# Even and odd rows in the filter's first transform, and Q's second half projected last

## The chip, the cores and the metric

The kernel runs on one core of one Trainium2 chip. The metric is the device time of one execution in microseconds. Durations of single instructions come from one profiled execution, whose page and trace are read below.

The core has five engines that run their own instruction lists and meet at semaphores: PE (TensorE, matmuls), ACT (ScalarE), DVE (VectorE), POOL (GpSimd) and SP (SyncE, which here only issues transfers).

## The reference

Two independent computations share one output row: 640 columns of a spectral filter (A) and 640 columns of attention (B).

```python
def _A_ref(x, w_r, w_i):                     # x: (1, 2048, 640); w: (2048, 321)
    X = rfft2(x.astype(float32), axes=(-2, -1))
    X = X * (w_r + 1j * w_i)
    return irfft2(X, s=(2048, 640), axes=(-2, -1)).astype(bfloat16)

def _B_ref(x, wqkv, wo):                     # H = 32 heads of Dh = 20
    q, k, v = heads(x @ wqkv)
    p = softmax(einsum("bhqd,bhkd->bhqk", q, k) * Dh ** -0.5)
    return merge(einsum("bhqk,bhkd->bhqd", p, v)) @ wo

return concatenate([a, b], axis=-1)          # (1, 2048, 1280)
```

## The kernel before

**Attention.** Queries are cut into four chunks of 512 (qc), heads into eight groups of four (g). One pair (qc, g) is a unit; there are 32 units, in the order of the list UNITS: the first 16 have qc 0 and 1, the last 16 have qc 2 and 3. Unit 8 is (0, 4), unit 10 is (0, 6). A unit has 16 key tiles times 4 heads = 64 score tiles, each one matmul of 32 rows by 512 columns (`score_mm`, L821), so there are 2048 score tiles in all. The exponential of a tile is taken on one of two engines. ScalarE takes two tiles in one instruction (L1418). VectorE makes an approximation from integer arithmetic in sets of four tiles (L955 out of PSUM, then L998 and L997 on the set, L1005 on V). P times V is L1076: four 32-column matmuls run side by side as one wave. At a unit's end the sum is copied out (L1107) and normalised by way of two small DRAM buffers `sd` and `rd` and a Pool multiplication (L1128); the heads are packed and projected by `wo` (L1222, and L1227 for the last two units).

**Projections of B.** x is transposed into `xT` (L592). Q and K for the first eight heads, except Q's queries of qc 2 and 3, are projected directly in the padded layout that the scores want (`proj0`, L614). All else is projected densely, 128 columns at a time (`packed`, L643): each of nine chunks (which, c) gives jobs of five matmuls per 512 rows, is evicted by VectorE (L655) into one of two staging buffers `stg`, and is copied from there by `spread_heads` into the padded `QT` and `KT`, one SyncE transfer per head part. The chunks alternate K and Q: (1,1), (0,1), (1,2), (0,2), (1,3), (0,3), (1,4), (0,4), each for all 2048 rows, and at last (0,0) for the second half of the rows. V is projected by L690.

**The filter.** Pool folds A's rows s and s + 1024 into sum and difference and columns likewise, and the result goes to DRAM as `xs` (`fold_x`). `jobs_A` then builds four stages of jobs. S1 (L1736) is the transform along rows: for each of even and odd frequencies and each of real and imaginary part, five jobs of eight matmuls of 512 columns, each evicted by one VectorE copy (L1742) into `X1`. S2 (L1793) transforms along columns and multiplies by the weights on VectorE (L1824, then combines at L1832 to L1841). S3 (L1896, evicted at L1910 to L1923) and S4 (L1948, evicted at L1956 and L1967) are the way back.

S1's input `xf` takes two transfers of 1.31 MB from `xs`, and its table takes four of 1.05 MB in two alternating buffers. The memory of `xf` is that of `xT`, that of the tables that of `stg`, and that of `X1` that of the weights `wqkv`. The keys ("z", "A"), ("z", "B") and ("z", "C") in the job lists stand for these regions, so S1's loads wait for the last job of the projections.

**What sets the order.** Each engine's instruction list is fixed when the program is built. A planner (`run`) walks in its own reckoned time: it fills score tiles for ScalarE first (`try_act_fill`), gives VectorE tiles by its backlog (`dve_wants`), and puts background jobs, ordered by `prio`, on PE where there is room (`try_bg`, `emit_chunk`). A job may not start before its due time `rel`. The filter's due times are spread from FT0 to FT1 in proportion to the PE work ahead of each job:

```python
J.prio = 2000.0 + n
J.rel = self.FT0 + (self.FT1 - self.FT0) * acc / tot
```

When there is too little work, the planner puts in filler matmuls (L1507). At run time each engine executes its list strictly in order, and waits at semaphores. SyncE's transfers too stand in one list.

A second computation for extreme inputs follows behind a flag; it is not executed with these inputs.

Of the kernel before, what the change touches and what calls it, by code (L numbers as in the profile page):

```python
# [297 lines left out]
class KB:  # L298
# [44 lines left out]
    def alloc(self):  # L343
# [48 lines left out]
        self.wqkv = a.bf(zB, 5 * 1920).rearrange("p (c n) -> p c n", c=5)  # L392
# [10 lines left out]
    def alloc_filter(self):  # L403
        a = self.ar
        zA, zB, zC, zD = self.zA, self.zB, self.zC, self.zD
        self.xf = [a.bf(zA + 10240 * i, 8 * 640).rearrange("p (t d) -> p t d", t=8) for i in range(2)]
# [3 lines left out]
        self.tabs = [a.bf(zC + 8192 * i, 8 * 512).rearrange("p (t k) -> p t k", t=8) for i in range(2)]  # L410
        self.X1 = a.bf(zB, 5 * 2 * 1024).rearrange("p (c r k) -> p c r k", c=5, r=2)
# [4 lines left out]
        self.FD = a.bf(zC, 4 * 3 * FBC).rearrange("p (m t l) -> p m t l", m=4, t=3)  # L416
        o = zC + 4 * 3 * FBC * 2
        self.Wb = [[a.bf(o + (2 * i + s) * 2 * FBC * 2, 2 * FBC).rearrange("p (r l) -> p r l", r=2) for s in range(2)] for i in range(2)]
        self.Wx = [[a.bf(zA + 2576 + (2 * i + s) * 2 * FBC * 2, 2 * FBC).rearrange("p (r l) -> p r l", r=2) for s in range(2)] for i in range(2)]
        self.TU = a.bf(zD, 4 * FBC).rearrange("p (s r l) -> p s r l", s=2, r=2)  # L420
        self.VX = a.bf(zD + 8 * FBC, 4 * FBC).rearrange("p (s r l) -> p s r l", s=2, r=2)
        self.X24 = a.bf(zD + 16 * FBC, 8)
# [83 lines left out]
    def setup_B(self):  # L506
# [28 lines left out]
        for c0, nm in ((640, "wk0"), (0, "wq0")):  # L535
            self.dma(self.wqkv[:, :, c0:c0 + 160], wv[:, :, c0:c0 + 160], 204800, w=[(nm,)], name="ld_" + nm)
# [5 lines left out]
        self.dma(self.wqkv[:, :, 1280:1920], wv[:, :, 1280:1920], 819200, r=[("xn", 0, 1)], w=[("wv",)], name="ld_wv")  # L542
        ld_x(2)
        ld_x(3)
        self.dma(self.wqkv[:, :, 800:1280], wv[:, :, 800:1280], 614400, r=[("xn", 0, 1)], w=[("wk",)], name="ld_wk")
        self.dma(self.wqkv[:, :, 160:640], wv[:, :, 160:640], 614400, r=[("xn", 0, 1)], w=[("wq",)], name="ld_wq")
        self.dma(self.sel, cFd.ap()[:, 0:85], 43520, r=[("xn", 0, 1)], w=[("sel",)], name="ld_sel")
        self.dma(self.ixt, self.c_ix.ap(), 4096, w=[("ixt",)], name="ld_ix", rel=60000.0)
        for g in range(2):
            for i in (1, 0):  # L550
                d_ = self.w0[g][i].rearrange("p c (j e) -> p c j e", e=32)[:, :, :, 0:20]
                s_ = self.wqkv[:, :, 640 * i + 80 * g: 640 * i + 80 * g + 80].rearrange("p c (j e) -> p c j e", e=20)
                self.dve_push([((lambda d_, s_: lambda e, en: e.tensor_copy(d_, s_))(d_, s_), 420.0, [("w0z",), (("wq0", "wk0")[i],)], [("w0", g, i)], [], "padw")],
                              prio=0 if g == 0 else 1)
# [23 lines left out]
    def jobs_B(self):  # L578
        ps, psb = self.ps, self.psb
        J = {}  # L580
        for i in range(4):
            for t2 in range(2):
                for gi, cbs in enumerate(((0, 1, 2), (3, 4))):
# [15 lines left out]
                    ev = [(mkev, 0.52 * n * 256 + 70, [("z", "A", 0)], [("xT", i, t2, gi)], [], True)]  # L599
# [5 lines left out]
        def proj0(g, which, kc):  # L605
# [3 lines left out]
            for c in range(5):  # L609
                def mk(bank, c=c):  # L610
                    o = ps[:, bank, :]
                    l = w0[:, c, :]
                    r_ = self.xT[:, c, kc * 512:(kc + 1) * 512]
                    return lambda e: e.matmul(o, l, r_, start=(c == 0), stop=(c == 4))  # L614
                pe.append((mk, 216.0, [("w0", g, which), ("z", "C", 0), ("z", "A", 0)] + xk(kc)))
# [19 lines left out]
        def packed(which, c, kc, sb, free):  # L635
            pe = []
            col = which * 640
            for cc in range(5):
                def mk(bank, cc=cc):
                    o = ps[:, bank, :]  # L640
                    l = self.wqkv[:, cc, col + c * 128: col + (c + 1) * 128]
# [7 lines left out]
                pe.append((mk, 216.0, wks + [("z", "B", 0), ("z", "A", 0)] + xk(kc) + (free if cc == 0 else [])))  # L649

            def mkev(bank):
                o = self.stg[sb][:, kc * 512:(kc + 1) * 512]
# [3 lines left out]
            ev = [(mkev, 610.0, [("z", "C", 0)], [("stg", which, c, kc)], [("stgb", sb, kc)], False)]  # L656
            return Job("pk%d" % which, 0.0, pe, ev)
        sb = 0
        hist = []
        order = [(1, 1), (0, 1), (1, 2), (0, 2), (1, 3), (0, 3), (1, 4), (0, 4), (0, 0)]  # L660
        for n_, (which, c) in enumerate(order):
                js = []
                free = hist[-2] if len(hist) >= 2 else []
                hist.append(self.spread_keys(which, c))
                for kc in (range(2, 4) if (which, c) == (0, 0) else range(4)):
                    j = packed(which, c, kc, sb, free)
                    j.prio = 1000.0 + 10 * n_ + kc
                    j.rel = self.PJ0 + self.PJ1 * (n_ + 0.25 * kc)
# [3 lines left out]
                def post(job, which=which, c=c, sb=sb, js=js):  # L672
                    if any(not x.done for x in js):
                        return
                    self.spread_heads(which, c, sb)
                for j in js:
                    j.post = post
                sb = (sb + 1) % 2
        for m in range(4):
            for k2 in range(8):  # L680
                pe = []
                for i in range(2):
                    kt = 2 * k2 + i
                    for c in range(5):
                        def mk(bank, c=c, kt=kt, i=i, m=m):
                            o = ps[:, bank, i * 160:(i + 1) * 160]
                            l = self.xT[:, c, kt * 128:(kt + 1) * 128]
                            r_ = self.wqkv[:, c, 1280 + m * 160: 1280 + (m + 1) * 160]
                            st = (c == 0 and i == 0)
                            return lambda e: e.matmul(o, l, r_, start=st, stop=(c == 4), skip_group_check=True)  # L690
                        pe.append((mk, 70.0, [("wv",), ("z", "B", 0), ("z", "A", 0)] + xk(kt // 4)))
# [16 lines left out]
    def spread_keys(self, which, c):  # L708
        nm = ("QT", "KT")[which]
        ks = []  # L710
        for h in range(H):
            lo, hi = max(20 * h, 128 * c), min(20 * h + 20, 128 * c + 128)
            if lo < hi and not (which == 1 and h < 8):
                ks.append((nm + "h", h, c))
        return ks

    def spread_heads(self, which, c, sb):
        dst = (self.QT, self.KT)[which]
        nm = ("QT", "KT")[which]
        for h in range(H):  # L720
            lo, hi = max(20 * h, 128 * c), min(20 * h + 20, 128 * c + 128)
            if lo >= hi:
                continue
            g, j = divmod(h, 4)
            s0 = 0
            if g < 2:
                if which == 1:
                    continue
                s0 = 1024
            d0 = 32 * j + lo - 20 * h  # L730
            o = dst[d0:d0 + hi - lo, g, s0:2048]
            i_ = self.stg[sb][lo - 128 * c: hi - 128 * c, s0:2048]
            self.dma(o, i_, (hi - lo) * (2048 - s0) * 2, r=[(nm + "m", g)] + [("stg", which, c, kc) for kc in range(s0 // 512, 4)] + [("stgb", sb, kc) for kc in range(s0 // 512, 4)] + [("z", "C", 0)],
                     w=[(nm + "h", h, c)], name="spread")

    def kq_keys(self, u, kt):
        qc, g = UNITS[u]
        if g < 2:
            ks = [("KT", g, kt // 4)]
            if qc < 2:  # L740
                ks.append(("QT", g, qc))
            else:
                ks += [("QTh", h, c) for h in range(4 * g, 4 * g + 4) for c in range(20 * h // 128, (20 * h + 19) // 128 + 1)]
            return ks
        ks = []
        for h in range(4 * g, 4 * g + 4):
            c0, c1 = 20 * h // 128, (20 * h + 19) // 128
            for c in range(c0, c1 + 1):
                ks += [("KTh", h, c), ("QTh", h, c)]
        return ks  # L750
# [868 lines left out]
    def fold_x(self):  # L1619
# [3 lines left out]
        for t in range(8):  # L1623
# [5 lines left out]
            k = [("fxl", t, 0), ("fxl", t, 1), ("fx", f, 0), ("fx", f, 1), D1, ("z", "C", 0)]  # L1629
            self.pool_op((lambda xa, xb: lambda e: e.tensor_tensor(a_, xa, xb, ALU.add))(xa, xb), 1600.0, r=k, w=[("ft", 0), D0] if t == 0 else [("ft", 0)], name="fold")  # L1630
            self.pool_op((lambda xa, xb: lambda e: e.tensor_tensor(b_, xa, xb, ALU.subtract))(xa, xb), 1500.0, r=k, w=[("ft", 1), D0] if t == 0 else [("ft", 1)], name="fold")
            for i, (src, dst) in enumerate(((a_, xa), (b_, xb))):
                lo, hi = src[:, 1:320], src[:, 321:640][:, ::-1]
                kk = [("ft", i), D1, ("z", "C", 0)]
# [3 lines left out]
                self.dma(self.xs[i][128 * t:128 * t + 128, :], dst, 163840, r=[("ff", t, i, q) for q in range(3)] + [("fx", f, i), ("z", "C", 0)], w=[("xs", i, t)], name="st_fx")  # L1638
# [3 lines left out]
    def filter_tables(self):  # L1642
# [5 lines left out]
        for par in range(2):  # L1648
            k = 2 * np.arange(512, dtype=np.int64) + par
            ang = th * ((s[:, None] * k[None, :]) % S)  # L1650
            c_, n_ = np.cos(ang), np.sin(ang)
            m_ = -n_
            if par == 0:
                m_[:, 0] = alt
            for m in (c_, m_):
                t1.append(m.reshape(8, 128, 512).transpose(1, 0, 2))
# [42 lines left out]
    def jobs_A(self, after, need):  # L1699
# [16 lines left out]
        def load_x():  # L1716
            for i in range(2):
                self.dma(self.xf[i], self.xs[i].rearrange("(t p) d -> p t d", p=128), 1310720, r=[("xs", i, t) for t in range(8)], w=[("xf", i), zr("A", 0)], name="ld_xA")
        def load_t(tabs, srcs, idx, ep, key, first_w):
            b = idx % 2  # L1720
            self.dma(tabs[b].rearrange("p t k -> p (t k)"), srcs[idx].ap(), 1048576, w=[(key, idx), (key + "b", b)] + first_w, name="ld_tab")
        hook("ldx", after, load_x, need)
        hook("ldt0", after, lambda: [load_t(self.tabs, self.c_t1, i, 1, "t1", [zr("C", 0)]) for i in range(2)], need + [("xs", i, t) for i in range(2) for t in range(5, 8)])
        S1 = []
        for idx in range(4):
            ri, par = idx % 2, idx // 2
            b = idx % 2
            js = []
            for c in range(5):
                pe = []  # L1730
                for t in range(8):
                    def mk(bank, t=t, c=c, par=par, b=b):
                        o = ps[:, bank, :]
                        l = self.xf[par][:, t, c * 128:(c + 1) * 128]
                        r_ = self.tabs[b][:, t, :]
                        return lambda e: e.matmul(o, l, r_, start=(t == 0), stop=(t == 7))  # L1736
                    pe.append((mk, 216.0, [("xf", par), ("t1", idx), ("t1b", b), zr("A", 1), zr("C", 1)]))

                def mkev(bank, c=c, ri=ri, par=par):
# [458 lines left out]
```

## Time and profile before

| | |
|---|---|
| median of 5 runs | 766.31 us (765.36 to 768.05) |
| the profiled execution: its own time, its span | 765.82 us, 764.0 us |
| TensorE's granted clock | 0.998 of full speed |
| busy: PE, DVE, ACT, POOL | 731.0, 667.6, 728.4, 133.7 us |
| bytes moved by DMA | 46.76 MB |

A row of the page's groups gives the line, the engine and operation, what is written and read, the shape, and the count; after the first bar the busy time and the mean of one instruction; after the second bar how long the engine sat idle just before these instructions, and what ended most of that. A row of the timeline gives the start and duration in microseconds, the same names, and in brackets the idle time ahead of it. Matmuls overlap, so a row's mean for PE is longer than the time between two of them. The span runs from the first to the last instruction; the execution's own time is a little longer.

### The profile page before, as it was taken

The numbers are of one execution on the slowest core, as the hardware profiler recorded it, in microseconds if no ns is written. First come the engines' busy times: TensorE is split into PE (matmuls) and PEld (weight loads), VectorE is DVE, ScalarE is ACT, GpSimd is POOL, SyncE is SP. The second block draws the span as 40 slices with busy tenths as digits, with TensorE's granted clock in tenths as the row PEclk, the third lists the DMA queues.
The fourth block names the chain that finished last, engine by engine and source line by source line (L and its number), as shares of the span: only waits on it lengthen the run. The fifth ranks groups of instructions, "written<-read, shape, count | busy, mean of one in ns | idle before, by whom it ended". The sixth has DMA issues, their size and how long they took to land.

```text
span 764.0 us, 16364 instructions
## 1 busy us (share of the span) xinstructions
PE 731.0 (96%) x6532; PEld 236.0 (31%) x6591; DVE 667.6 (87%) x1234; ACT 728.4 (95%) x797; POOL 133.7 (17%) x142
## 2 busy tenths in 40 slices
PE   8999999999999999999999999999999999999997
PEld 4422242232422222232222333332232322333334
DVE  3598989888888989888989999999998889899895
ACT  5899999999799999999999999999999999999992
POOL 7287940000000000003000211210001000000000
PEclk9999999999999999999999999999999999999999
DMA  9022330210202442013121111212001110211102
GB/s 307 16 72 89 92 117 25 45 46 21 64 25 58 147 150 76 20 46 113 25 69 30 54 33 35 53 38 94 24 19 48 37 31 21 71 56 37 54 19 72
DMA packets 43009, 46.76 MB, mean 61 GB/s; under 512 B 16470, under 2 KB 36312, under 8 KB 42416
## 3 DMA queue, kind: packets, MB, share of 16 engines
q1 hardware_dynamic: 42160, 44.35, 19.4%
q0 software_dynamic: 768, 1.32, 0.7%
q8 instruction: 53, 0.87, 0.5%
q14 instruction: 28, 0.23, 0.1%
HBM read 30.57 MB, written 8.36 MB: 51 GB/s over the span
## 4 chain that ended last, share of the span: by engine, by line
ACT 47%; PE 43%; DVE 7%; issue 1%; DMA 1%; SPq 0%
ACT arena L1418 46%; PE ps L821 14%; PE ps L1076 11%; PE ps L643 4%; DVE arena L955 3%; PE ps L1736 3%; PE ps L1222 2%; PE ps L1793 2%; PE ps L690 2%; PE ps L614 2%; PE ps L1896 1%; DVE arena L998 1%; DMA arena<-ct 1%; DVE arena L997 1%; PE ps L1948 1%
## 5 line engine op out<-in xcount | busy, mean ns | idle before, releaser
L1418 ACT ACTIVATE arena<-ps 128x1024 f16<-128x1024 f32 x784 | 721.2, 1121 | 13.0 <-PE ps L821 10.5
L955 DVE TENSOR_SCALAR arena<-ps 128x512 int16<-128x512 f32 x480 | 320.0, 682 | 44.6 <-PE ps L821 42.4
L821 PE MATMUL ps<-arena 32*128 32x512 bf16 x2048 | 307.9, 384 | 13.4 <-ACT arena L1418 9.0
L1076 PE MATMUL ps<-arena 128*32 128x512 f16 x3008 | 234.9, 385 | 1.7 <-DVE arena L998 0.6
L821 PEld LDWEIGHTS ps<-arena 32*128 32x128 bf16 x2048 | 76.0, 91 | 296.8 <-ACT arena L1418 275.9
L1128 POOL TENSOR_TENSOR arena<-arena 128x512 bf16<-128x512 f32 x30 | 39.8, 1327 | 493.6 <-DMA arena<-rd 493.6
L998 DVE TENSOR_SCALAR arena<-arena 128x2048 int16<-128x2048 int16 x120 | 89.1, 742 | 1.4
L997 DVE TENSOR_SCALAR arena<-arena 128x2048 int16<-128x2048 int16 x120 | 85.4, 712 | 3.1 <-PE ps L1076 2.3
L1076 PEld LDWEIGHTS ps<-arena 128*32 128x32 bf16 x3008 | 50.3, 94 | 95.2 <-issue 65.9
L643 PE MATMUL ps<-arena 128*128 128x512 bf16 x149 | 44.8, 383 | 2.2 <-issue 1.8
L1736 PE MATMUL ps<-arena 128*128 128x512 bf16 x140 | 41.8, 383 | 3.5 <-issue 2.4
L1793 PE MATMUL ps<-arena 128*128 128x322 bf16 (+1 forms) x198 | 37.7, 303 | 0.2 <-DVE arena L955 0.2
L1948 PE MATMUL ps<-arena 128*128 128x320 bf16 (+1 forms) x192 | 34.8, 302 | 0.1
L1896 PE MATMUL ps<-arena 128*128 128x512 bf16 (+3 forms) x121 | 29.8, 332 | 1.9 <-issue 1.3
L690 PE MATMUL ps<-arena 128*128 128x160 bf16 x320 | 30.1, 234 | 1.3 <-DVE arena L955 1.2
L1005 DVE TENSOR_SCALAR arena<-arena 128x96 bf16<-128x96 bf16 x120 | 30.5, 255 | 0.0
L1824 DVE TENSOR_TENSOR arena<-ps,arena 128x644 bf16<-128x644 f32 (+1 forms) x34 | 27.9, 821 | 2.2 <-PE ps L1793 1.7
L1222 PE MATMUL ps<-arena 128*128 128x320 bf16 (+1 forms) x152 | 28.2, 302 | 0.8 <-DVE arena L955 0.5
L655 DVE TENSOR_SCALAR arena<-ps 128x512 bf16<-128x512 f32 x34 | 23.1, 679 | 2.8 <-PE ps L643 2.5
L690 PEld LDWEIGHTS ps<-arena 128*128 128x128 bf16 x320 | 21.5, 98 | 12.5 <-issue 9.8
L696 DVE CAST arena<-ps 128x320 bf16<-128x320 f32 x32 | 15.4, 488 | 10.6 <-PE ps L690 10.4
L1107 DVE COPY arena<-ps 128x512 f32<-128x512 f32 (+1 forms) x33 | 21.9, 666 | 1.5 <-PE ps L1076 1.4
(77 smaller groups left out, 355.5 us busy)
## 6 DMA issues: line engine op xcount, KB each, us to landing
arena<-rd SPq DMA_DIRECT2D x120, 64.0 KB
out_dram<-arena SPq DMA_DIRECT2D x32, 160.0 KB
arena<-ct SPq DMA_DIRECT2D x4, 1024.0 KB
arena<-arena SPq DMA_DIRECT2D x42, 80.0 KB
arena<-in_A_x_dram SPq DMA_DIRECT2D x16, 160.0 KB
xs<-arena SPq DMA_DIRECT2D x16, 160.0 KB
arena<-xs SPq DMA_DIRECT2D x2, 1280.0 KB
arena<-arena SPq DMA_DIRECT2D x105, 20.0 KB
```

What stands on the lines that cost most here:

```text
L643: return lambda e: e.matmul(o, l, r_, start=(cc == 0), stop=(cc == 4))
L690: return lambda e: e.matmul(o, l, r_, start=st, stop=(c == 4), skip_group_check=True)
L821: return e.matmul(self.ps[:, bank, :], self.KT[32 * j:32 * j + 32, g, kt * 128:(kt + 1) * 128], self.QT[32 * j:32 * j + 32, g, qc * 512:(q ...
L955: return e.tensor_scalar(o, in_, 0.0, 31744.0, ALU.max, ALU.min)
L997: self.dve_push([(lambda e, en: e.tensor_scalar(Ii, Ii, SH2, 0.0, ALU.subtract, ALU.max), occ, ik + pk, ik, [], "p3")], lambda: push(self. ...
L998: ops = [(lambda e, en: e.tensor_scalar(Gi, Ii, SH1, 0.0, ALU.subtract, ALU.max), occ, ik, [("G", b)], [], "p2")]
L1076: inst = e.matmul(self.ps[32 * j:32 * j + 32, bank, :], v_, p_, start=s_, stop=False, tile_position=(0, 32 * j), skip_group_check=True)
L1222: return lambda e: e.matmul(o, ot[0:M, c, qb * 128:(qb + 1) * 128], self.wo[0:M, c, half * 320:(half + 1) * 320], start=(c == 0), stop=(c ...
L1418: self.put("act", lambda e: e.activation(o, in_, AF.Exp, bias=ACT_BIAS, scale=ACT_SCALE), 0.8333 * 512 * n + 60.0, r=[("ps", b) for b in b ...
L1736: return lambda e: e.matmul(o, l, r_, start=(t == 0), stop=(t == 7))
L1793: return lambda e: e.matmul(o, lhs, r_, start=st, stop=sp)
L1948: return lambda e: e.matmul(o, l, r_, start=(n == 0), stop=(n == 5))
```

## The change

There are four parts.

1. **S1 by even and odd rows.** The 1024 folded rows are split into even and odd ones. A job is now four matmuls of 512 columns, of which 256 are real and 256 imaginary parts, for half the frequencies of before. For each of five column chunks c and each parity there are two jobs, even rows (e = 0) and odd rows (e = 1). The even job's result is copied to an f32 buffer `sb1`; the odd job's result is added to it for the first 256 frequencies and subtracted from it, written in reversed order, for the others. In even parity three one-column operations follow for the middle frequency and `X24`. The reversed half has the imaginary part's sign turned, which S2 takes up in its choice of tables (`neg`). The tables shrink from four to two.

2. **Q's second half last.** The order of the staged chunks becomes K for all rows, then Q for the first 1024 rows, for c = 1 to 4, and then Q for the last 1024 rows for c = 0 to 4. The staging slots are tracked one by one, and the keys of Q's copies get a half as fourth part.

3. **The first load ahead.** The weights are kept as two tensors, `wkv` and `wq`, with zone keys B and B2, the halves of `xT` get A and A2, and the tables' regions C2 and C. The loads for even parity (`load_1(0)`) are released by all projection jobs but Q's second half (`early`), and those for odd parity by all of them. The input is loaded in ten transfers of 128 KB a parity, in the layout (c, i, t, d), so that each parity lies in the half of `xT`'s memory that is free by then; it was one of 1280 KB.

4. **The filter's due times.** FT1 goes from 745000 to 700000.

The core of the diff:

```diff
-        order = [(1, 1), (0, 1), (1, 2), (0, 2), (1, 3), (0, 3), (1, 4), (0, 4), (0, 0)]
+        for c in range(1, 5):
+            order += [(1, c, (0, 1, 2, 3), 0, 0), (0, c, (0, 1), 1, 2 * (c % 2))]
+        order += [(0, c, (2, 3)) + sl for c, sl in enumerate(((1, 2), (0, 0), (0, 2), (1, 0), (1, 2)))]
...
+        def load_1(i):
+            v = self.xs[i].rearrange("(t p e) (c d) -> e p t c d", p=128, e=2, d=128)
+            for e in range(2):
+                for c in range(5):
+                    self.dma(self.xf[i][:, c, 4 * e:4 * e + 4, :], v[e][:, :, c, :], 131072, r=[("xs", i, t) for t in range(8)], w=[("xf", i, e, c)],
+                             pw=[("xf", i), zr(("A", "A2")[i], 0)], name="ld_xA")
+            self.dma(self.tabs[i].rearrange("p t k -> p (t k)"), self.c_t1[i].ap(), 1048576, w=[("t1", i), ("t1b", i)], pw=[zr(("C2", "C")[i], 0)], name="ld_tab")
...
+        hook("ldx0", early, lambda: load_1(0), xsk)
+        hook("ldx1", after, lambda: load_1(1), need + xsk)
...
-        for idx in range(4):
-            ri, par = idx % 2, idx // 2
-                for t in range(8):
-                        return lambda e: e.matmul(o, l, r_, start=(t == 0), stop=(t == 7))
-                    return lambda e, en: e.tensor_copy(o, in_)
+        for par in range(2):
+            for c in range(5):
+                for e in range(2):
+                    for n in range(4):
+                            return lambda e: e.matmul(o, l, r_, start=(n == 0), stop=(n == 3))
+                    if e == 0:
+                            return lambda e, en: e.tensor_copy(sb1, ps[:, bank, :])
+                    else:
+                            return lambda e, en: e.tensor_tensor(X[:, :, 0:256], ps[:, bank, :].rearrange("p (r k) -> p r k", r=2), sv, ALU.add)
...
+                            return lambda e, en: e.tensor_tensor(X[:, :, 511:255:-1], sv, i_, ALU.subtract)
...
-    FT1 = 745000.0
+    FT1 = 700000.0
...
+        early = [J for k, J in self.jB.items() if not (k[0] == "pk" and k[1] == 0 and k[3] >= 2)]
+        self.jobs_A(early, pk, need)
```

## The prediction

> **What bounds the kernel now.** I read the page's busy table first, then the groups, then ScalarE's own timeline, since the groups name ScalarE's exp as the work everything else feeds.
>
> ```profile
> PE 731.0 (96%) x6532; PEld 236.0 (31%) x6591; DVE 667.6 (87%) x1234; ACT 728.4 (95%) x797; POOL 133.7 (17%) x142
> L1418 ACT ACTIVATE arena<-ps 128x1024 f16<-128x1024 f32 x784 | 721.2, 1121 | 13.0 <-PE ps L821 10.5
> L955 DVE TENSOR_SCALAR arena<-ps 128x512 int16<-128x512 f32 x480 | 320.0, 682 | 44.6 <-PE ps L821 42.4
> ```
>
> PE and ACT both look full, so the shares alone do not choose. The second line does: 784 exp instructions cost 721.2 us, and ACT was idle before them for only 13.0. VectorE idled 44.6 us for score tiles, so it has room. ScalarE's timeline (start, duration, group, idle before it):
>
> ```profile
> 13.76 14.77 ACT L1418 ACTIVATE arena<-ps 128x1024 f16<-128x1024 f32 x16 [0.49 <-PE ps L821]
> 29.57 5.61 ACT L1418 ACTIVATE arena<-ps 128x1024 f16<-128x1024 f32 x6 [1.04 <-PE ps L821]
> 37.46 55.32 ACT L1418 ACTIVATE arena<-ps 128x1024 f16<-128x1024 f32 x60 [2.29 <-PE ps L821]
> ...
> 207.13 62.44 ACT L1418 ACTIVATE arena<-ps 128x1024 f16<-128x1024 f32 x68 [3.92 <-PE ps L821]
> ...
> 505.18 68.00 ACT L1418 ACTIVATE arena<-ps 128x1024 f16<-128x1024 f32 x74 [1.77 <-PE ps L1076]
> 734.46 13.08 ACT L1418 ACTIVATE arena<-ps 128x1024 f16<-128x1024 f32 x14
> ```
>
> So the 764.0 us span is a sum of four terms: 13.8 before the first exp, 721.2 of exp, 12.5 of gaps between exps (13.0 less the 0.49 before the first), and 16.5 from the last exp's end (734.46 + 13.08 = 747.5) to the end. A change pays only in the gaps or in the two ends, or by moving tiles off ScalarE. The largest gap and the tail, in the timeline of all engines:
>
> ```profile
> 203.76 3.01 PE L690 MATMUL ps<-arena 128*128 128x160 bf16 x41
> 755.18 4.26 PE L1948 MATMUL ps<-arena 128*128 128x320 bf16 x30
> 759.48 1.01 DVE L1967 TENSOR_TENSOR arena<-arena,ps 128x320 bf16<-128x320 f32 x2
> ```
>
> At 202.4 to 206.7 PE runs V projections (L690) with no score (L821) among them. This is where attention unit 8 begins, whose Q and K come from staged chunk 3, the sixth of nine; its seven copies lie among 12 SyncE transfers issued only from 198.85 to 207.98. At the end, 30 matmuls of the filter's last stage run alone after attention's output is done.
>
> **What the Trainium skill says.** "Perfetto Trace Analysis", Identifying the Most-Contended Engine, says matmul busy share is a poor measure, while occupancy is fair for ScalarE. The trace agrees: PE shows 96%, yet a 320-column matmul listed at 302 ns is issued every 137 ns in the run of 30 (4.11 us in the chain of waits). "TensorE: Matmul & The Clock Gate", Back-to-back issue gap, gives N/2.4 + 2.5 ns, so 136 and 216 for 320 and 512 columns; ten L614 matmuls took 2.33 us, 217 apart after the last one's 380. "VectorE: DVE Perf Modes", Why PSUM operands drop a tier, holds fp32 from PSUM to the slowest mode: here copy (L1742, 681 ns) and add or reversed subtract with PSUM (L1918, L1923, 682 and 679) cost the same. "DMA: Bandwidth & Descriptors", Why small descriptors are slow, matters for the new 256-byte runs, priced below.
>
> **The change, part by part.** Instruction counts and places come from the two programs' instruction orders side by side; a place is how many of the 2048 score tiles were issued before it. One tile is 734/2048 = 0.358 us.
>
> *ScalarE's work.* 784 exps in both orders, and 480 VectorE tiles in both. So 721.2 stays. PE's order is unchanged up to tile 191, so the head stays 13.8, and so do the gaps 1.04 and 2.29.
>
> *Row transform.* 160 matmuls of 512 columns become 80: 80 x 0.217 = 17.4 us less PE. PE does not set the end by itself, so I count it at nothing; what it buys is room in which later filter work can be placed. VectorE: 20 evictions become 10 copies, 10 adds, 10 reversed subtracts (30 x 0.681) and 15 one-column operations (0.15 each, as L1913): +9.1 us. Covered by its 44.6 idle, but packed into tiles 694 to 833, 50 us, where VectorE gets 22.7 us of this beside its exp share. If that cover is gone, PE waits for a bank and ScalarE for PE. The nearest stage of that density, the filter's second (L1824 and its combines, 43.8 us in 79), shows 2.5 us of gaps. I take 0.8, bounds 0 to 3. One Pool copy goes: nothing.
>
> *Q's second half last.* 170 projection matmuls in both. Unit 8's operands are now the 90th projection matmul, at tile 451, rather than the 120th at 508. The run of 51 V matmuls between two scores is gone: minus 3.9. Next late would be unit 10, from tile 640 on: its 120th matmul is issued at 576, so I add nothing, bound 2.
>
> *Clumps.* The longest PE work between two scores, after tile 191, is now 7 transform matmuls and 3 waves of P x V at tile 788: 7 x 0.217 + 12 x 0.054 = 2.2 us. Before, clumps of 4.46, 2.72 and 1.57 gave gaps of 3.92, 2.29 and 1.04, each about 0.5 less: so plus 1.6. The clump behind the 1.77 gap (12 P x V and 6 of L1793, with a late VectorE copy) is gone, as is 0.27 at 269.8, the wait for the table: minus 2.0. The smaller gaps stay, among them 1.35 at 93 to 97, where VectorE's L998 took 1.45 instead of 0.74 beside Pool.
>
> *Loads.* SyncE issues 27 more staged copies (90 for 63), 18 more loads (20 of 128 KB for 2 of 1280) and 2 table loads fewer: 27 x 0.76 + 18 x 0.4 - 2 x 0.35 = 27 us more of SyncE time, in a queue that waits over 250 us for others' results. Behind them stand the normalisation transfers of a unit, needed two units (46 us) later. The first loads now stand before unit 8's end, some 40 us ahead of use: hidden. The second set follows the last projection at tile 694 and is needed at 772: 78 x 0.358 = 28 us. Its 5120 runs of 256 bytes: the two early 320-byte loads moved 1377 small packets in 2.0 us (window 4.3 to 6.3), so 7.4 us, plus a table of 3 and issue: about 14. Hidden; the page's 27% penalty at 256 bytes would not change that.
>
> *Tail.* The filter's last matmul now comes at tile 1938, so the 30 are gone: minus 4.1, and minus 0.5 because one eviction, not two, is left behind the last matmul. 8 instead of 20 P x V matmuls follow the last score: minus 0.6. Tail 16.5 - 5.2 = 11.3; bounds 10.5 and 12. The store's 3.5 stays.
>
> Sum: gaps 12.5 - 3.9 - 2.0 + 1.6 + 0.8 = 9.0; 13.8 + 721.2 + 9.0 + 11.3 = **755.3 span**. The profiled execution took 765.82 for a span of 764.0, and the median, 766.31, is 0.5 above it: 755.3 + 1.8 + 0.5 = **757.6**.
>
> **Rivals.** (a) *The gaps come back.* VectorE's extra 9.1 us arrives in the busiest stretch, the stage before it showed waits there, and the gaps end where they were. For it: the 1.77 gap was PE behind a VectorE copy. Against it: PE holds fewer matmuls in that stretch. Only the tail pays: 766.3 - 5.2 = 761.1, to 763.3 with 2.2 more lost.
> (b) *Slower: the second set of loads is late at tile 772.* PE, in order, stops at the first transform matmul of the odd half, and scores queue behind it. It costs nothing up to 28 us of loading, then a microsecond each. It decides the sign when it eats the 8.7 gained: beyond 37 us, and beyond 39 it is slower by over 0.3%. That needs packets about five times the price above. At 42 us: 757.6 + 14 = 771.6. The measured small packets speak against it.
> (c) *The tail is not shorter*, because ending the filter earlier only moves work before the last exp and each piece delays a score: 757.6 + 5 = 762.6. Against it: the last two units have little filter work left, and even ten filler matmuls.
>
> **How the numbers follow.** My forecast 0.80, (a) 0.10, (b) 0.05, (c) 0.05. Best: no new gaps, 6.6, and a tail of 10.5: 752.1 + 2.3 = 754.4. Worst of (a) 763.3. Range 754 to 763.3. A measurement of this kernel tells about 0.3%, 2.3 us, from no change: same is 764.0 to 768.6. (a) reaches it about one time in three, and (c) also, giving 0.05 with a little of (b): faster 0.89, same 0.05, slower 0.06.
>
> **What would show it.** 784 exps at 721; no gap of 3 us near 200; ScalarE gaps after tile 126, that is after 60 us, of 4 to 8 in all; one new gap near 290; no L1948 counterpart after the last exp, and 11 us from there to the end. Wrong if PE waits for transfers of xs or a table, if VectorE waits move into 255 to 310 us, or if exps number fewer.

## The result, and the profile after

The changed kernel takes 767.27 us in the median of 26 runs (764.17 to 770.23), the kernel before 766.32 us in 47 runs beside it; the ratio, taken over all these runs and not from the two medians, is 1.0004 with an interval of 0.9992 to 1.0016. That is no change. The forecast was 757.6, with a range of 754.0 to 763.3, so the time lies above the range.

The page of the changed kernel, its busy table, the clock by fortieths of the span, and the two groups of exponentials:

```profile
PE 723.6 (95%) x6469; PEld 231.0 (30%) x6513; DVE 665.2 (87%) x1259; ACT 729.7 (96%) x797; POOL 133.8 (18%) x141
...
PEclk9999999999999798999999999999999999999999
...
L1409 ACT ACTIVATE arena<-ps 128x1024 f16<-128x1024 f32 x784 | 722.6, 1117 | 17.6 <-PE ps L812 15.1
L946 DVE TENSOR_SCALAR arena<-ps 128x512 int16<-128x512 f32 x480 | 319.7, 681 | 31.8 <-PE ps L812 29.6
```

Again 784 exponentials, for 722.6 us, but the idle time before them rose from 13.0 to 17.6, and the clock has two dents, in slices 14 and 16 (248 to 267 and 286 to 306 us). VectorE waited less for scores than before (29.6 for 42.4). ScalarE's timeline (start, duration, group, idle time ahead of it and what ended it) says where the idle time lies:

```profile
98.05 150.11 ACT L1409 ACTIVATE arena<-ps 128x1024 f16<-128x1024 f32 x163 [0.44 <-PE ps L812]
251.85 1.02 ACT L1409 ACTIVATE arena<-ps 128x1024 f16<-128x1024 f32 x1 [3.70 <-PE ps L812]
253.36 1.02 ACT L1409 ACTIVATE arena<-ps 128x1024 f16<-128x1024 f32 x1 [0.48 <-PE ps L812]
254.87 1.03 ACT L1409 ACTIVATE arena<-ps 128x1024 f16<-128x1024 f32 x1 [0.48 <-PE ps L812]
256.93 2.11 ACT L1409 ACTIVATE arena<-ps 128x1024 f16<-128x1024 f32 x2 [1.03 <-PE ps L812]
259.51 36.16 ACT L1409 ACTIVATE arena<-ps 128x1024 f16<-128x1024 f32 x39 [0.47 <-PE ps L812]
297.39 1.02 ACT L1409 ACTIVATE arena<-ps 128x1024 f16<-128x1024 f32 x1 [1.73 <-PE ps L812]
...
310.79 265.77 ACT L1409 ACTIVATE arena<-ps 128x1024 f16<-128x1024 f32 x289 [1.69 <-PE ps L1067]
576.75 176.33 ACT L1409 ACTIVATE arena<-ps 128x1024 f16<-128x1024 f32 x192 [0.19 <-PE ps L812]
```

The stall of 3.92 near 203 us is gone: the row at 98.05 runs through it. The last exponential ends at 576.75 + 176.33 = 753.1, and 10.8 us follow it, where there were 16.5. Both gains were forecast. Against them stand two new clusters of gaps: 3.70 + 0.48 + 0.48 + 1.03 + 0.47 = 6.2 us from 248 on, and five of 4.3 us together from 295.7 on (the first is shown; 0.82, 0.49, 0.91 and 0.34 follow). The 1.69 at 310.79 is the one new gap that was forecast.

What stopped PE at 248, in the timeline of all engines:

```profile
248.87 0.25 DVE L1113 RECIPROCAL arena<-arena 128x16 f32<-128x16 f32 x1 [4.04 <-DMA arena<-sd]
249.81 1.46 PE L645 MATMUL ps<-arena 128*128 128x512 bf16 x3 [2.95 <-DVE arena L946]
```

The reciprocal (L1113, L1122 before) is a quarter of a microsecond of work in the normalisation of a finished unit. It stood at the head of VectorE's list for 4.04 us, waiting for a transfer from `sd`. Behind it in that list stood exponentials that would have freed a bank of PSUM, the memory that matmuls write to, so PE waited 2.95 us, and so ScalarE. The transfer is the end of a short chain: `norm_dma` stores the sums of a unit to `sd` (four transfers), loads them back in another layout, and VectorE inverts them. SyncE's timeline shows why it was late:

```profile
216.68 9.19 SPq L483 DMA_DIRECT2D arena<-arena  x12
225.92 1.03 SPq L483 DMA_DIRECT2D arena<-xs  x2
227.00 5.20 SPq L483 DMA_DIRECT2D arena<-arena  x7
232.24 4.33 SPq L483 DMA_DIRECT2D arena<-xs  x8
236.61 0.51 SPq L483 DMA_DIRECT2D arena<-ct  x1
237.16 5.53 SPq L483 DMA_DIRECT2D arena<-arena  x7
242.79 1.23 SPq L483 DMA_DIRECT2D sd<-arena  x4
244.12 3.01 SPq L483 DMA_DIRECT2D arena<-arena  x4
247.31 0.36 SPq L483 DMA_DIRECT2D arena<-sd  x1
```

Read each row's end against the next row's start: SyncE issues without a pause. The sums were ready at 229.5 (VectorE's copy L1098, 0.68 us from 228.84), but their stores left at 242.79, 13.3 us later, behind the rest of the seven staged copies of 227.00, eight loads of xs, a table and seven more copies; the reload then stood behind four more copies. From 216.6 to 288.8 SyncE's rows add up to 68.7 of 72.2 us, where in the kernel before they add up to 43.7. The Trainium skill, "Perfetto Trace Analysis", What "DMA-bound" means, lists this as a bound of its own: the issuing engine's track is solid with DMA slices, which are the making of descriptors and not data on the move. The trace agrees: 0.75 us of issue per staged copy, most of them of 20 to 80 KB, while the DMA engines were 0.40 busy from 216 to 292.

The second cluster begins in the same way, but has a part more. SyncE's rows, and VectorE's:

```profile
287.55 1.17 SPq L483 DMA_DIRECT2D sd<-arena  x4
292.57 0.36 SPq L483 DMA_DIRECT2D arena<-sd  x1
294.25 0.25 DVE L1113 RECIPROCAL arena<-arena 128x16 f32<-128x16 f32 x1 [2.68 <-DMA arena<-sd]
```

These sums were ready at 280.7 (VectorE's copy from 279.99) and left 6.9 us later, behind staged copies, loads and the second table. Then 3.9 us passed between the last store (288.72) and the reload, with SyncE idle; in the kernel before it was 0.9 (235.86 to 236.78). The table had been issued just ahead of these stores, and the DMA engines were 0.67 busy in those 3.9 us. So here the data on the move adds to SyncE's delay; e6 below shows which of the two makes the stall.

Then PE's clock. Stretches of the same trace; the columns are PE, PEld, DVE, ACT and Pool busy (instructions), granted clock, DMA share and GB/s:

```profile
247.00:251.00 4.00, 1.19 (x3) 0.28 (x3) 2.13 (x6) 1.16 (x2) 0.00 (x0) 0.69 0.23 52
251.00:259.00 8.00, 8.00 (x39) 1.45 (x38) 3.82 (x6) 5.08 (x5) 1.27 (x1) 0.51 0.25 65
259.00:285.00 26.00, 24.97 (x214) 6.92 (x214) 23.07 (x48) 25.47 (x29) 1.28 (x1) 1.00 0.26 62
295.00:303.00 8.00, 6.97 (x33) 1.40 (x34) 4.80 (x13) 4.06 (x5) 1.26 (x1) 0.58 0.11 35
```

After the stop PE was busy all the time and issued 39 matmuls in 8 us, where it issues 66 in 8 us from 259 on. The granted clock was 0.51. That is what turns one gap of 3.70 into 6.2 us.

### The profile page after: what moved, and what is told of

Read it like the earlier page. It is cut to its first block, busy times and chain, and to the rows that moved or that the text cites. A ratio compares the mean times of both kernels' runs of the same rounds, so it can differ in the third digit from the quotient of the medians.

```text
span 763.9 us, 16311 instructions
## 1 busy us (share of the span) xinstructions
PE 723.6 (95%) x6469; PEld 231.0 (30%) x6513; DVE 665.2 (87%) x1259; ACT 729.7 (96%) x797; POOL 133.8 (18%) x141
## 3 DMA queue, kind: packets, MB, share of 16 engines
q0 software_dynamic: 768, 1.32, 0.7%
## 4 chain that ended last, share of the span: by engine, by line
ACT 60%; PE 31%; DVE 6%; issue 1%; DMA 1%; SPq 0%
ACT arena L1409 59%; PE ps L812 11%; PE ps L1067 8%; PE ps L645 4%; DVE arena L946 3%; PE ps L694 2%; PE ps L617 2%; PE ps L1734 2%; DVE arena L988 1%; PE ps L1213 1%; PE ps L575 1%; DVE arena L989 1%; DMA sd<-arena 1%; ACT arena L601 0%; DMA arena<-sd 0%
## 5 line engine op out<-in xcount | busy, mean ns | idle before, releaser
L1409 ACT ACTIVATE arena<-ps 128x1024 f16<-128x1024 f32 x784 | 722.6, 1117 | 17.6 <-PE ps L812 15.1
L946 DVE TENSOR_SCALAR arena<-ps 128x512 int16<-128x512 f32 x480 | 319.7, 681 | 31.8 <-PE ps L812 29.6
L812 PE MATMUL ps<-arena 32*128 32x512 bf16 x2048 | 310.3, 387 | 22.8 <-ACT arena L1409 16.5
L645 PE MATMUL ps<-arena 128*128 128x512 bf16 x149 | 47.1, 397 | 5.8 <-DVE arena L946 3.3
L1972 PE MATMUL ps<-arena 128*128 128x320 bf16 (+1 forms) x192 | 36.6, 302 | 0.2 <-DVE arena L946 0.2
L694 PE MATMUL ps<-arena 128*128 128x160 bf16 x320 | 31.7, 234 | 0.5 <-DVE arena L946 0.4
L1098 DVE COPY arena<-ps 128x512 f32<-128x512 f32 (+1 forms) x33 | 21.9, 667 | 8.6 <-PE ps L1067 8.2
L1213 PE MATMUL ps<-arena 128*128 128x320 bf16 (+1 forms) x152 | 28.9, 302 | 0.3 <-DVE arena L1751 0.3
L996 DVE TENSOR_SCALAR arena<-arena 128x96 bf16<-128x96 bf16 x120 | 26.3, 219 | 0.0
L1734 PE MATMUL ps<-arena 128*128 128x512 bf16 x73 | 22.9, 401 | 0.9 <-issue 0.8
```

The source lines that it names most:

```text
L645: return lambda e: e.matmul(o, l, r_, start=(cc == 0), stop=(cc == 4))
L812: return e.matmul(self.ps[:, bank, :], self.KT[32 * j:32 * j + 32, g, kt * 128:(kt + 1) * 128], self.QT[32 * j:32 * j + 32, g, qc * 512:(q ...
L946: return e.tensor_scalar(o, in_, 0.0, 31744.0, ALU.max, ALU.min)
L1409: self.put("act", lambda e: e.activation(o, in_, AF.Exp, bias=ACT_BIAS, scale=ACT_SCALE), 0.8333 * 512 * n + 60.0, r=[("ps", b) for b in b ...
L1734: return lambda e: e.matmul(o, l, r_, start=(n == 0), stop=(n == 3))
L1972: return lambda e: e.matmul(o, l, r_, start=(n == 0), stop=(n == 5))
```

## The experiments

**Theory A:** SyncE is saturated from 216 to 292 us, the sums leave late, and a reciprocal in VectorE's list stops VectorE, PE and ScalarE in turn. **Theory B:** the row transform's added VectorE work, or its denser stage, starves PE. The text of e2 adds a rival C: the data of the new loads, moving on the DMA engines, make the sums late. Ratios are to the kernel before, run on the same chip.

**e1: the reciprocal later.** A step after planning moves three reciprocals.

```diff
         self.run()
+        self.rec_later((8, 9, 10), 12)
```

> The changed kernel with one thing moved: the softmax reciprocals of units 8, 9 and 10 (L1113) stand 12 places later in VectorE's list; PE, ScalarE and SyncE keep their lists. Theory A (SyncE is backlogged from 217 to 292 us, so the sums return late, the reciprocal blocks VectorE's in-order list for 4.0 and 2.7 us, PE waits for a bank, ScalarE starves and PE's clock falls): both stalls go, about 12 us of ScalarE gaps with them, time about 755 to 757 us. Rival B (the stalls come from PE itself, from too little work and the lower clock, or from VectorE being full in the new row transform): nothing changes, 766 to 768.

765.35 us (20 runs), ratio 0.9988 (0.9973 to 1.0002): the time that A gave is missed. The gap at 248 is gone, and another came 26 us later, in the timeline of all engines:

```profile
273.47 0.36 SPq L483 DMA_DIRECT2D arena<-sd  x1
275.07 0.25 DVE L1113 RECIPROCAL arena<-arena 128x16 f32<-128x16 f32 x1 [4.35 <-DMA arena<-sd]
276.52 1.03 PE L1734 MATMUL ps<-arena 128*128 128x512 bf16 x2 [3.80 <-DVE arena L946]
278.14 1.02 ACT L1409 ACTIVATE arena<-ps 128x1024 f16<-128x1024 f32 x1 [4.29 <-PE ps L812]
```

The same engines stop in the same order at the next unit, whose reciprocal was moved too. SyncE's list has the store of the inverted sums (to `rd`), which waits for the reciprocal: with the reciprocal later, SyncE stood still for 3.7 us (251.9 to 255.65), and all that stood behind left later still. Moving the reciprocals does not help while the queue ahead of the sums is full.

**e2: the loads off SyncE.** The 20 loads of xs and the two tables are issued by Pool.

```diff
+        mv = [t for t in P.order["sp"] if t.name in ("ld_xA",) or (t.name == "ld_tab" and t.gidx < cut)]
+        q = P.order["pool"] + mv
```

> The changed kernel with the 20 input loads and 2 tables of the row transform issued from Pool's queue instead of SyncE's; every other list the same. Theory A: the sums of unit 8 are issued about 6 us earlier (the loads and the table ahead of them took 1.0 + 4.3 + 0.5 us on SyncE), the reciprocal no longer waits 4.0 us, the first stall goes and most of the second: 755 to 760 us. Rival B: 766 to 768. Rival C (the data of the loads on the DMA engines, not SyncE's issue time, make the sums late): the second stall, beside xs and the table, stays: 760 to 763.

760.89 us (5 runs), ratio 0.9927 (0.9902 to 0.9952). The number is C's, and 0.9 above A's range. One stall is left (VectorE's waits, then ScalarE's timeline):

```profile
DVE arena L1113 <- DMA arena<-sd: 5.9, 2, 4.4
```

```profile
269.19 1.02 ACT L1409 ACTIVATE arena<-ps 128x1024 f16<-128x1024 f32 x1 [3.40 <-PE ps L812]
```

Of the waits of 8.2 us at L1113 in the changed kernel 5.9 are left, and 6.4 us of time came back in the medians. It is not the stall that C said would stay: the reciprocal beside the second set of loads (at 290.1) did not wait. The one that did, at 266.9, waited for sums whose stores left at 256.20 and 260.81 and whose reload left at 265.10, with ten staged copies between. The loads are part of the backlog and not all of it.

**e3: a plan that knows SyncE's price.** The planner reckons 450 ns of SyncE for every transfer.

```diff
-        self.free["sp"] = st + 450.0
+        occ = 760.0 if name == "spread" else 550.0 if name == "ld_xA" else 450.0
+        self.free["sp"] = st + occ
```

> The changed kernel, planned with 760 ns of SyncE time for a staged copy and 550 for an input load instead of 450. All lists are planned anew. Theory A: the planner then puts the reciprocal where its data are there, no VectorE wait of over 1 us at L1113, 755 to 759 us. Rival B: no effect beyond 1 us, 765 to 769.

765.93 us (20 runs, 761.04 to 768.88), ratio 0.9995 (0.9978 to 1.0013). In the profiled execution, one of the shorter (762.39), the waits at the reciprocal (L1114 here) fell to 5.2 us in three, but ScalarE got a gap of 2.72 at 288 and a dozen smaller ones spread over the span. A better estimate moved the stall about; it takes no issue off the queue. This run changes every engine's list, so it tells A and B apart poorly.

**e5 and e6: Q's second half on Pool's queue.** In e6 the 45 staging copies of Q's last 1024 rows are issued by Pool, and all other lists stay; e5 moves the 20 loads and two tables as well.

```diff
-                     w=[("KTh", h, c) if which else ("QTh", h, c, kcs[0] // 2)], name="spread")
+                     w=[("KTh", h, c) if which else ("QTh", h, c, kcs[0] // 2)], name="spread" if kcs[0] < 2 else "spread2")
...
+        mv = [t for t in P.order["sp"] if t.name == "spread2"]
+        q = P.order["pool"] + mv
```

> The changed kernel with the row transform's loads and the 45 staged copies of Q's second half issued from Pool's queue; every other list the same. Moving the loads alone left one ScalarE stall of 4.2 us, at 265 us, where a reciprocal waits for sums that SyncE issued behind copies of Q's second half. Theory A (SyncE's backlog): that stall goes too, no reciprocal waits over 1 us, 755 to 758 us. Rival D (Q's second half stalls the kernel by its extra data or its place on PE, not by SyncE): 760 to 762 as with the loads alone.

> The changed kernel with only the 45 staged copies of Q's second half on Pool's queue, the loads on SyncE. SyncE is rid of some 30 us of issue between 237 and 285 us, but the first ten loads and the table still stand ahead of unit 8's sums. Theory A: the first stall shrinks to less than half or goes, the second, where the sums share SyncE and the DMA engines with the second set of loads, may stay: 757 to 762 us. If the loads are the whole cause, 765 to 768.

e6 takes 756.5 us (4 runs, 753.82 to 758.71), ratio 0.988 (0.9849 to 0.991); e5 756.75 us (4 runs), ratio 0.9878 (0.985 to 0.9906). Both beat both kernels, and moving the loads as well adds nothing. ScalarE's timeline of e6:

```profile
36.73 231.89 ACT L1409 ACTIVATE arena<-ps 128x1024 f16<-128x1024 f32 x252 [2.29 <-PE ps L812]
269.08 27.07 ACT L1409 ACTIVATE arena<-ps 128x1024 f16<-128x1024 f32 x29 [0.46 <-PE ps L812]
...
410.89 329.96 ACT L1409 ACTIVATE arena<-ps 128x1024 f16<-128x1024 f32 x359 [0.18 <-PE ps L812]
```

252 exponentials run in one row where the changed kernel stopped at 248. The row transform and all its VectorE work are unchanged here, so B falls; so does rival D, since the data of Q's second half and its place on PE are unchanged too. SyncE's timeline, and Pool's:

```profile
235.86 1.12 SPq L483 DMA_DIRECT2D sd<-arena  x4
241.38 0.35 SPq L483 DMA_DIRECT2D arena<-sd  x1
```

```profile
227.54 4.51 POOL L483 DMA_DIRECT2D arena<-arena  x7 [11.80 <-DVE arena L657]
```

The same stores leave 8.0 us after their copy instead of 13.3, and the reload 13.6 us after it instead of 17.8; this reciprocal does not wait (one wait of 1.3 us is left at a reciprocal in the whole run). Nor does the one beside the second set of loads, though those still move: its stores again took 3.9 us until the reload (275.97 to 279.89), but they had left 1.9 us after their copy instead of 6.9. So C's delay is there, and without SyncE's it made no stall. SyncE's rows from 216.6 to 288.8 add up to 41.9 us.

**e8 and e9: late sums put into the kernel before.** If A is right, the old kernel must stall when only its sums are made late. 24 small transfers are put on SyncE's queue ahead of the sums of unit 13. In e8 they wait only for the data that they read, in e9 also for the copy that the sums wait for.

```diff
         self.run()
+        self.busy_sp(13)
...
-                j.deps = [d for d in P.bufs[("ident",)].writers]
+                j.deps = list(t.deps)
```

> The kernel before with 24 idle transfers of 5 KB (20 rows of the identity to a scratch tensor in DRAM) put on SyncE just ahead of unit 13's sums, near 320 us, and all other lists unchanged: some 9 us of SyncE time, nothing else. Theory A: the reciprocal of unit 13 then waits 4 to 7 us at the head of VectorE's list, ScalarE gaps of 3 to 9 us follow, PE's granted clock drops, and the time rises by 4 to 9 us, to 770 to 775. If normalisation had the slack of two units that I gave it: 766.

> The kernel before, with 24 small transfers of 5 KB (20 rows of the identity into a scratch tensor in HBM, read by nobody) put on SyncE's queue directly ahead of the four sum transfers of unit 13, and made to wait for the same copy of the sums that those wait for, so that they cannot run early as they did in the first form of this experiment. The lists of PE, VectorE, ScalarE and Pool are those of the kernel before. At 0.37 us of issue each, as measured in that first form, the sums leave about 9 us late. Theory A (a reciprocal that stands in VectorE's in-order list waits for late sums, VectorE stops, PE waits for a bank, ScalarE starves): one wait of 3 to 7 us at the reciprocal (L1122), a ScalarE gap of 2 to 5 us followed by several of 0.5 to 1 us, a dip of the granted clock, and 769 to 775 us. Theory B (late sums are absorbed; the time went to VectorE's 9 us of added work): no wait at L1122, 766 to 767.5 us.

e8: 767.49 us (20 runs), ratio 1.0013 (1.0002 to 1.0025), a miss for A's number. Its transfers began at 338.13, before the sums were ready at 343.3, so the sums left only 3.9 us late and the reciprocal waited 1.1. e9: 773.34 us (6 runs), ratio 1.0084 (1.0058 to 1.0109). All engines of e9:

```profile
341.69 9.66 SPq L2171 DMA_DIRECT2D junk<-arena  x24
351.39 1.14 SPq L480 DMA_DIRECT2D sd<-arena  x4
353.45 0.34 SPq L480 DMA_DIRECT2D arena<-sd  x1
355.02 0.25 DVE L1122 RECIPROCAL arena<-arena 128x16 f32<-128x16 f32 x1 [6.84 <-DMA arena<-sd]
355.96 0.60 PE L821 MATMUL ps<-arena 32*128 32x512 bf16 x1 [4.81 <-DVE arena L955]
358.12 1.94 ACT L1418 ACTIVATE arena<-ps 128x1024 f16<-128x1024 f32 x2 [5.76 <-PE ps L821]
```

The whole chain of the changed kernel stands here in the old one, with nothing changed but SyncE's queue: 9.7 us of delay, 6.84 at the reciprocal, 5.76 at ScalarE, then gaps of 0.43, 0.48 and 0.27 at a clock of 0.73 (358 to 366). Together 6.9 us of gaps; the span grew from 764.0 to 771.8. Both runs give the slack of that reciprocal, the time by which its sums may be late at no cost: 3.9 - 1.1 and 9.7 - 6.8, that is 2.8 and 2.9 us.

**e4, e7 and e10: the due time.** e4 puts FT1 back to 745000 in the changed kernel, e10 does so with e6's queues, and e7 sets 700000 in the kernel before.

```diff
-    FT1 = 700000.0
+    FT1 = 745000.0
```

> The changed kernel with the filter's last due time back at 745 us. The stalls near 250 and 297 us stay; matmuls of the filter's last stage come back behind the last exp, so the tail grows from 10.8 to 14 to 16 us: 770 to 772 us. If the shorter tail came from the smaller row transform and not from the due times, 766 to 768.

> The kernel before with one part of the change alone: the filter's last due time at 700 instead of 745 us. If the due time alone makes the tail short, the 30 matmuls leave it and 761 to 763 us result. If the room for them comes from the smaller row transform, the 17 us of PE work still to be placed delay scores before the last exp: 764 to 768 us.

> The changed kernel with the 45 staging copies of Q's second half on Pool's queue, as in the run e6, and in addition the filter's due time FT1 back at 745000. What it tells is the worth of the due time once the stall of SyncE is gone. If the tail is shortened by the due time (forecast: 16.5 to 11.3 us, of which 4.6 for the filter's last matmuls), the filter's last-stage matmuls stand after the last exp again: tail 14 to 16 us, 759.5 to 762 us. If the room that the smaller row transform leaves is what ends the filter early, and the due time is idle: 756 to 757.5 us, no such matmuls behind the last exp.

e4: 773.56 us (10 runs), ratio 1.0095 (1.0073 to 1.0117), above the range that was given. e10: 762.07 us (7 runs), ratio 0.9937 (0.9912 to 0.9961), above e6 by 5.6 us in the medians and 4.4 by the ratios. e7: 766.28 us (20 runs), ratio 1.0005 (0.999 to 1.002). PE's timeline of e4, and of e7:

```profile
765.85 1.80 PE L1972 MATMUL ps<-arena 128*128 128x320 bf16 x12
```

```profile
753.17 4.25 PE L1948 MATMUL ps<-arena 128*128 128x320 bf16 x30
```

With the old due time filter matmuls stand behind the last exponential again. In e4 it ended at 758.8 and 13.9 us followed, 3.1 more than in the changed kernel; 786 exponentials took 725.4, 2.8 more, and their gaps were 3.0 longer. In the kernel before, the new due time leaves every engine's list as it was, and the 30 matmuls stay: the due time was not what held that filter back. So the short tail needs the due time and the smaller row transform (with its earlier loads) together; e11 and e12 below, which have these two and not the split of Q, have tails of 11.7 and 11.8 us.

**e11 and e12: Q whole again.** In e11 the chunks and their order are those of the kernel before, with 63 copies on SyncE; row transform, loads and FT1 are the new ones. e12 also puts the loads and tables on Pool's queue, as e2.

```diff
-            order += [(1, c, (0, 1, 2, 3), 0, 0), (0, c, (0, 1), 1, 2 * (c % 2))]
-        order += [(0, c, (2, 3)) + sl for c, sl in enumerate(((1, 2), (0, 0), (0, 2), (1, 0), (1, 2)))]
+            order += [(1, c, (0, 1, 2, 3), 0, 0), (0, c, (0, 1, 2, 3), 1, 0)]
+        order += [(0, 0, (2, 3), 0, 2)]
```

> The changed kernel with the Q chunks projected whole again, in the chunk order of the kernel before (63 staging copies on SyncE instead of 90, chunk 3 sixth); the row transform by even and odd rows, its 20 loads on SyncE, and the due time 700000 stay. Theory A (SyncE's backlog of copies and loads makes the sums late): 27 x 0.75 = 20 us less issue between 216 and 292 us, so no wait at the reciprocal, or one below 2 us; the stall of about 3.9 us near 203 us comes back since unit 8's operands are again the 120th projection matmul; the tail stays short; 759 to 763 us. Theory B (the row transform's added VectorE work is what takes the gain): the stalls between 245 and 312 us stay, and with that of 203 us back the time is 769 to 772 us.

> The kernel of e11 (Q projected whole, 63 staging copies on SyncE, row transform by even and odd rows, due time 700000) with the 20 loads of xs and the two tables issued from Pool's queue instead of SyncE's; PE, VectorE and ScalarE keep e11's lists. In e11 one reciprocal wait of 4.3 us remained, at sums that SyncE issued at 267.85 behind a run of loads and copies. Theory A (SyncE's backlog, here made by the loads alone): 22 issues, about 12 us, leave SyncE's stage, so no wait at the reciprocal, no gap near 278; the 3.92 gap near 207 stays, since unit 8's operands are still the 120th projection matmul; 759 to 762 us. Theory B (the added VectorE work of the row transform starves PE whatever SyncE does): a gap of 2 us or more stays between 245 and 312 us, 764 us or more.

e11: 768.97 us (20 runs), ratio 1.0033 (1.0015 to 1.0051). e12: 766.43 us (20 runs), ratio 1.0007 (0.9991 to 1.0024). Both times miss what A gave and lie where B put them (769 to 772, and 764 or more); the traces say why. In both the stall of 3.9 near 203 us is back, so that gain was the split's. In e11 a reciprocal waited 4.3 us, and ScalarE 4.48 at 278.6: the 20 loads among the old number of copies are enough to make sums late. In e12 these sums left 6.8 us after their copy instead of 12.7, and no reciprocal waited, as A said, but ScalarE's timeline has a new gap, and PE's waits name it:

```profile
251.91 1.94 ACT L1414 ACTIVATE arena<-ps 128x1024 f16<-128x1024 f32 x2 [2.85 <-PE ps L817]
```

```profile
PE ps L817 <- DMA arena<-arena: 3.0, 1, 3.0
```

A score waits for a staged copy. Some 245 exponentials are done by then, and 245/784 of 2048 tiles is tile 640, the start of unit 10. SyncE was hardly later with this unit's chunk than in the kernel before, where no score waited: it issued seven copies from 241.05 to 246.89, there from 240.35 to 246.42. What differs is the data beside them: Pool had issued the first table at 241.45, which took 9.2 us to land, and the DMA engines were 0.84 busy from 244 to 248, for 0.45 in the kernel before. So this wait points to the loads' data, as in C; no run here shows it by taking them away. The gap is not VectorE's, so e12 gives B nothing; but neither run is a clean test of one part, since the orders differ.

## Why the prediction was wrong

*What held.* 784 exponentials; head 13.4 for 13.8; the stall near 203 gone (minus 3.9, confirmed by its return in e11 and e12); the 1.77 gap gone; one new gap of 1.69 for a forecast 1.6; tail 10.8 for 11.3. For the price of a matmul, the Trainium skill, "TensorE: Matmul & The Clock Gate", Back-to-back issue gap, calls the formula used that of a single matmul and gives about 131 ns for a stream of 512-column ones; ten in a row were 217 ns apart, so the measurement stands with the 216 that was used. VectorE's added work, priced at 0.8 us of gaps, cost none that is seen: outside the two clusters the gaps add up to 17.1 - 10.5 = 6.6 us, where 9.0 were forecast. Part of this is luck: the gaps of 1.35 us at 93 to 97, which the forecast kept, came to 0.44 in this execution.

*The step that failed* is "Loads". Its count (27 more copies, 18 more loads, two tables fewer, 27 us) was fair: from 216.6 to 288.8 alone the measured rows differ by 68.7 - 43.7 = 25 us. It failed in two sentences. SyncE's added time was set against "a queue that waits over 250 us for others' results", which is a sum over the whole span, while these 25 us fall into 72 us, which then have 3.5 us to spare. And the transfers behind it, "needed two units (46 us) later", were costed at nothing. The result of normalisation may be needed that late, but its reciprocal is in VectorE's in-order list, and the whole engine needs it when it comes up: within 2.9 us of slack at the unit that e8 and e9 tried, and about 12 at the first stall (an estimate: 13.3 us until the stores and 2.4 for the copies ahead of the reload, less the wait of 4.0), where 46 were reckoned. The rule to name who is queued behind a waiting instruction was applied to PE (rival b) and not to VectorE.

*The sum.* The span is 763.9 for 755.3: gaps 17.1 for 9.0 (two clusters of 10.5, the others 2.4 less; after 60 us 13.8, where 4 to 8 were named), exponentials 1.4 more, head and tail 0.9 less. e6 takes the term away and gives 13.0 + 721.1 + 6.7 + 11.2 = 752.0 of span, in an execution that was the lowest of its four; its median of 756.5 stands 1.1 below the forecast. So the working was right but for one term of 10.5 us, and that term was more than the whole gain. VectorE's waits moving into 255 to 310 us were named as what would refute the forecast: the second of the two (291.6 to 294.3) did, and the first (244.8 to 248.9) stood just ahead of that stretch.

*The rivals.* (a) said that the gaps come back and only the tail pays, by VectorE's work, at 761.1 to 763.3. Gaps came back through SyncE, and were longer than that. (b) did not occur, no matmul waited for a load of xs; the "about five times" in it is about four by its own numbers (37 us less 6.6 for table and issue, over 7.4). (c), a tail no shorter, is wrong for the whole change, and right for e7, the due time alone.

## What to carry to other kernels

When a change adds transfers, lay the issuing engine's timeline over the stage in which they are issued, and add the new issues there; a queue's idle time over the span says nothing of it. Then ask of each transfer behind them which engine's list has an instruction that waits for it: even a small operation off the critical path stops all that stands behind it in an in-order list. If the issuing engine is solid, move whole groups to another queue (here 45 copies, from 1.0004 to 0.988 of the kernel before) before moving the waiting instruction.

## What the runs showed of the hardware

A short stop of PE can cost more than its length, since a stretch of half clock follows. After the 2.95 us of waiting at 247 the granted clock was 0.50 from 248.6 to 258.7, and a gap of 3.70 became 6.2; after 1.32 us at 294.4 it was 0.50 from 296.3 to 303.1, and 1.73 became 4.3. In e9 4.81 us of waiting gave a gap of 5.76 and 1.2 more. The Trainium skill, "TensorE: Matmul & The Clock Gate", What's actually happening, says that about 3.4 us without activity bring the array to half its clock, and as long a stretch of work brings it back. Half is what the trace shows. But the clock fell here 1.7 us after the last matmul ahead of the stop, and in a stop shorter than 3.4 us, and the way back took longer: 8.9 us after PE had resumed. A dip can also come without such a stop. In e10 (stretches, columns as above):

```profile
674.00:678.00 4.00, 3.12 (x28) 0.95 (x27) 3.63 (x7) 4.00 (x5) 1.27 (x1) 1.00 0.26 91
678.00:684.00 6.00, 6.00 (x41) 1.27 (x38) 4.69 (x9) 3.78 (x5) 0.00 (x0) 0.57 0.06 16
```

PE was busy for 3.12 of the 4 us ahead, and its longest wait there was 0.40. That execution took 768.07 us, the other six of e10 761.01 to 762.36; what set off the dip stays open.

The cost of an issue hardly depended on its size: 0.5 us on SyncE for a load of 128 KB, 0.5 and 0.3 for the two tables of 1 MB, 0.75 for a staged copy of 40 KB. Pool issued the same copies in 0.5 to 0.65 us, and the loads in 0.8 (e2).
